# A lambda-shaped attention followed by a SoLU mixture layer: the last unit's feed-forward input side whole, its output side in halves with tiles of their own, and a new order of all steps

## The chip, the cores and the metric

The kernel runs on one core of one Trainium2 chip. Its time is the device time of one execution in microseconds (us); lower is better. The core has five engines that work side by side, each taking its own instructions in order: PE (matrix products and transposes), DVE (elementwise work on vectors), ACT (activation functions, with a scale and a bias), POOL (elementwise work, slower for most of it) and SP (it only issues transfers). ACT and POOL can issue transfers too. SBUF is the memory of 128 partitions that all engines read and write; PSUM is the small one that PE writes its results to.

## What is computed

Attention over 4 sequences of 768 positions with 8 heads of width 64, then a feed-forward layer of 1024 inner columns on the 3072 rows of 512 columns that come out. Of each row of scores only 8 global columns and the last 96 positions are kept, and each head has a bias that falls off with distance:

```python
scores = scale * np.matmul(q, k.transpose(0, 1, 3, 2))
is_global = pos[None, :] < int(n_global)              # n_global = 8
is_local = (rel >= 0) & (rel < int(n_local))          # n_local = 96
scores = scores + bias[None, :, :, :]                 # -slope of the head * distance
scores = np.where(is_global | is_local, scores, -1000000000.0)
a = np.exp(scores - max); a = a / (sum + 1e-09); x = a @ v
h = x @ w_in
solu = h * softmax(h)
ln = (solu - mean) / sqrt(var + 1e-06) * g_ln
out = ln @ w_out
```

## The kernel before

**Units and rows.** The 3072 rows are cut into 12 units of 256: unit u is sequence u // 3 and stretch u % 3 of it. A unit has two halves r of 128 rows in the feed-forward part.

**The order is written out.** The string ORDER lists 670 steps, one word each, and the kernel issues them in that order; nothing is rescheduled. Each engine gets its own instructions in the order of the words, and an engine that waits holds everything of its own that stands behind. A word is a name and its arguments; the letter after the name is the engine or the issuing queue (S is SP, A ACT, P POOL, D DVE). The pools of tiles give out slots when a step asks for a tile, and that step waits until the slot's last reader is done. What holds work up most is in PSUM: three slots called big, for scores (sc), sums (lb), values (pa) and the inner columns (ph), and two called small, for transposes (qturned, kturned, lT), global scores (gs), outputs (po), pv and the warm-up products.

**The attention steps of a unit.** `q`, `k`, `v` load 256 KB halves into 13 staging slots; `cq`, `ck`, `cv` cast them to 16 bits (cast, lines 138, 140 and 142 for ACT, DVE, POOL); `tq`, `tk` transpose on PE (L301) and `eq`, `ek` copy the result out of PSUM; `gk` picks the global keys (POOL, L315). `S:u:g` are the scores of a pair of heads (L324), `X` their exponentials on ACT (L333), `M` the product with the mask on DVE (L340), `gS` and `gX` the same for the global columns (L353, L361), `gv0` and `gv` the global values (POOL L366; PE L370 and DVE L373). `L` sums on PE (L384, L393), `I` inverts the sums on ACT in two instructions (L401, L402), `V` multiplies by the values (L412, L422) and `N` normalises into xT on DVE (L430).

**The feed-forward steps of half r of unit u.** `A:u:r` is the product with w_in into ph (L446, 8 products of 512 columns), `E` its exponential on ACT with the sum s0 (L460), `U` e times ph on DVE with the sum s1 (L468), `Q` the sum of squares s2 on ACT (L477), `Z` the scale rs from s0, s1 and s2 in five small POOL instructions (L492 to L499), `d` the transpose of un by a transfer on SP's queue into uT (L516; three slots), `O` the product with the scaled w_out into po (L522), `o` the scaling of po by rs into osb on DVE (L534) or ACT (L536), `st` the store (L543), whole units of 512 KB but for unit 11. w_out is loaded with `wo`, scaled with `sc`, its mean is taken (`mean`, `cm`) and removed (`ce` on DVE, L578; `pr` and `sm` on POOL, L590 and L594). `warm:n` are n products of zeros on PE (L230) that nothing reads.

**The last unit.** Unit 11 is worked in halves throughout: A, E, U and Q have a third argument, the half of the 1024 inner columns; its transposes go over PE (`t`, L505) and a copy (`e`) instead of a transfer; its outputs are stored in quarter units. The halves of one step write two halves of the same tile (one ph, one e, one un, one lT, one uT, one osb). Z then first adds the two partial sums of each kind (L488).

The units end in the order 8, 7, 11, 10, 9: the last words are those of unit 9's outputs and stores, with 18 warm-up products after the last output.

Of the kernel before, what the change touches and what calls it, by code (L numbers as in the profile page):

```python
# [26 lines left out]
q:S:0:0 k:S:1:0 k:S:0:0 off:1 off:0 zero dist:1 mask:1:0 mask:1:4 id cap dist:0 mask:0:2 mask:0:1  # L27
mask:0:5 mask:0:4 k:S:0:1 ck:P:0 tk:0 ek:D:0 q:S:0:1 cq:P:0 tq:0 k:S:1:1 ck:P:1 q:S:1:0 gb tk:1
ek:D:1 q:S:1:1 q:S:2:0 q:S:2:1 cq:D:2 mask:1:5 mask:0:0 mask:1:1 mask:0:6 mask:1:6 mask:1:3 eq:A:0
mask:0:3 S:0:0 gk:0 S:0:2 gS:0 X:0:0 X:0:2 S:0:3 k:S:3:0 S:0:1 X:0:1 cq:P:1 gX:0 fill hm X:0:3  # L30
k:S:2:0 k:S:2:1 ck:P:2 mask:1:7 mask:1:2 mask:0:7 tq:1 eq:D:1 tq:2 S:1:2 X:1:2 S:1:0 X:1:0 eq:D:2
M:0:3 gS:1 M:0:0 gX:1 S:1:1 X:1:1 v:S:0:0 S:1:3 tk:2 ek:A:2 q:S:4:0 q:S:4:1 cq:D:4 v:S:0:1 M:1:0
selV X:1:3 k:S:3:1 ck:D:3 wi:0 M:0:1 S:2:1 X:2:1 S:2:3 X:2:3 cv:P:0 S:2:0 gS:2 gX:2 gv0:0 X:2:0
M:0:2 M:1:2 S:2:2 k:S:4:0 k:S:4:1 tq:4 eq:A:4 M:1:3 tk:3 ek:D:3 gk:1 ck:A:4 X:2:2 L:0 I:0 M:1:1
# [629 lines left out]
```

The softmax here doesn't subtract the row's maximum and nothing guards it: scores larger than these inputs give would overflow.

## Time and profile before

| | |
|---|---|
| time, median of 3 runs | 174.66 us (174.57 to 175.02) |
| the profiled execution: its own time | 174.96 us |
| its span, first to last instruction | 173.2 us |
| busy: PE, ACT, DVE, POOL | 154.9, 144.5, 127.3, 91.4 us |
| granted PE clock over the span | 0.98 |
| moved by transfers | 34.35 MB, mean 198 GB/s |
| first transpose on PE; first product of the feed-forward part (A:0:0) | 8.00 us; 36.2 us |
| end of the last output (O:9:1); last store landed; last warm-up product ended | 168.4; 171.85; 172.3 us |

The busy shares are over the whole span. PE is busy almost without a break between 36 and 168 us, so what counts there is PE's idle time and what PE is given to do that nothing reads. A step's place in the trace is found by counting its instructions on its engine.

### The profile page before, as it was taken

How to read it: one execution, taken by the hardware profiler on the slowest of the kernel's cores; microseconds unless marked ns; L12 is line 12 of the kernel's file. 1: busy time of each engine (PE TensorE's matmuls, PEld its weight loads, DVE VectorE, ACT ScalarE, POOL GpSimd, SP SyncE). 2: the span in 40 equal slices, each digit the busy share in tenths (PEclk: the TensorE clock that was granted, in tenths of full speed). 3: DMA queues.
4: the chain of work that ended last, by engine and by line, in shares of the span. 5: the costliest groups of instructions: out<-in, count | busy, mean ns of one | idle time of the engine just before them, and what ended most of it. 6: DMA issues, size and time to landing. Idle time of an engine off the chain costs nothing.

```text
span 173.2 us, 4093 instructions
## 1 busy us (share of the span) xinstructions
PE 154.9 (89%) x1551; PEld 86.1 (50%) x1551; DVE 127.3 (73%) x200; ACT 144.5 (83%) x232; POOL 91.4 (53%) x195
## 2 busy tenths in 40 slices
PE   0179599899999989997999999999999958998997
PEld 0156375655654545436455655555545634454443
DVE  5079978999899989929989899869837672475310
ACT  5959999899999997769999899999895566796540
POOL 5276809300814998987288987882210001464760
PEclk9999759999999999999999999999999999999999
DMA  4999999999999998689999692398753530055354
GB/s 138 309 346 310 328 255 244 256 354 287 312 341 162 221 109 166 111 249 234 360 206 155 147 217 98 121 264 224 167 140 74 169 125 0 0 164 139 68 162 198
DMA packets 52532, 34.35 MB, mean 198 GB/s; under 512 B 43169, under 2 KB 43681, under 8 KB 52513
## 3 DMA queue, kind: packets, MB, share of 16 engines
q1 hardware_dynamic: 48784, 27.14, 63.9%
q0 software_dynamic: 1984, 5.77, 13.9%
q10 hardware_dynamic: 1744, 1.18, 2.5%
q8 instruction: 12, 0.20, 0.5%
q14 instruction: 8, 0.06, 0.1%
HBM read 23.07 MB, written 6.29 MB: 169 GB/s over the span
## 4 chain that ended last, share of the span: by engine, by line
PE 66%; POOL 10%; DVE 5%; DMA 5%; ACT 5%; issue 5%; SPq 4%; POOLq 0%; DVEq 0%; ACTq 0%
PE ph L446 21%; PE po L522 20%; PE lb L393 5%; PE pa L412 4%; PE warm L230 4%; SPq L157 4%; PE sc L324 3%; DMA q<-in_q_dram 3%; PE qturned L301 3%; POOL gw L594 2%; DMA v<-in_v_dram 2%; PE kturned L301 2%; DVE q L140 2%; ACT pt L333 2%; PE pa L422 1%
## 5 line engine op out<-in xcount | busy, mean ns | idle before, releaser
L446 PE MATMUL ph<-w_in,xT 128*128 128x512 f16 x192 | 44.9, 379 | 3.1 <-DVE un L468 2.3
L522 PE MATMUL po<-gw,uT 128*128 128x512 f16 x192 | 44.5, 379 | 0.0
L333 ACT ACTIVATE pt<-sc 128x896 f16<-128x896 f32 (+1 forms) x48 | 40.0, 871 | 2.2 <-PE sc L324 2.0
L468 DVE SCALAR_TENSOR_TENSOR un<-e,ph 128x1024 f16<-128x1024 f16 (+1 forms) x26 | 29.1, 1135 | 8.5 <-ACT e L460 7.6
L340 DVE TENSOR_TENSOR pt<-pt,mask 128x896 f16<-128x896 f16 (+1 forms) x48 | 28.3, 614 | 5.5 <-ACT pt L333 5.5
L446 PEld LDWEIGHTS <-xT 128*128 128x128 f16 x192 | 17.8, 98 | 24.0 <-issue 2.6
L460 ACT ACTIVATE e<-ph 128x1024 f16<-128x1024 f32 (+1 forms) x26 | 24.8, 955 | 4.5 <-PE ph L446 2.8
L522 PEld LDWEIGHTS <-uT 128*128 128x128 f16 x192 | 17.9, 98 | 20.9 <-issue 0.5
L477 ACT ACTIVATE sq<-un 128x1024 f16<-128x1024 f16 (+1 forms) x26 | 25.7, 990 | 2.0 <-DVE un L468 1.8
L497 POOL TENSOR_SCALAR w<-s,w 128x1 f32<-128x1 f32 x22 | 6.8, 311 | 32.3 <-ACT sq L477 30.6
L324 PE MATMUL sc<-qT,kT 64*128 64x128 f16 (+2 forms) x256 | 15.9, 246 | 3.0 <-ACT kT L138 1.8
L430 DVE TENSOR_TENSOR xT<-pa,rlb 128x1024 f16<-128x1024 f32 x12 | 14.6, 1221 | 2.9 <-ACT rlb L402 1.6
L301 PE MATMUL kturned<-ident,k 128*128 128x128 f16 x96 | 8.8, 246 | 8.0 <-POOL k L142 8.0
L495 POOL TENSOR_SCALAR w<-mean,w 128x1 f32<-128x1 f32 x24 | 14.5, 605 | 2.4
L499 POOL TENSOR_TENSOR rs<-w,neghalf 128x1 f32<-128x1 f32 x24 | 14.6, 610 | 2.0
L140 DVE COPY kT<-kturned 128x1024 f16<-128x1024 f16 x9 | 11.0, 1222 | 6.0 <-PE kturned L301 6.0
L534 DVE TENSOR_SCALAR osb<-po,rs 128x512 f32<-128x512 f32 (+1 forms) x15 | 10.7, 711 | 5.8 <-DMA out_dram<-osb 3.0
L401 ACT ACTIVATE rlb<-lb 128x1024 f32<-128x1024 f32 x12 | 12.4, 1032 | 3.0 <-PE lb L393 2.8
L536 ACT ACTIVATE osb<-po,rs 128x512 f32<-128x512 f32 (+1 forms) x11 | 7.1, 650 | 8.5 <-PE po L522 4.5
L324 PEld LDWEIGHTS <-kT 64*128 64x128 f16 x256 | 9.3, 100 | 8.3 <-issue 4.6
L402 ACT ACTIVATE rlb<-rlb 128x1024 f32<-128x1024 f32 x12 | 12.7, 1057 | 0.4
L301 PEld LDWEIGHTS <-k 128*128 128x128 f16 x96 | 7.1, 111 | 10.1 <-POOL k L142 8.2
(88 smaller groups left out, 230.2 us busy)
## 6 DMA issues: line engine op xcount, KB each, us to landing
out_dram<-osb SPq DMA_DIRECT2D x11, 512.0 KB, 2.9
q<-in_q_dram SPq DMA_DIRECT2D x19, 256.0 KB, 5.2
k<-in_k_dram SPq DMA_DIRECT2D x18, 256.0 KB, 5.3
v<-in_v_dram SPq DMA_DIRECT2D x16, 256.0 KB, 6.3
v<-in_v_dram POOLq DMA_DIRECT2D x7, 256.0 KB, 5.0
k<-in_k_dram POOLq DMA_DIRECT2D x6, 256.0 KB, 8.2
w_out<-in_moe_w_out_dram SPq DMA_DIRECT2D x3, 512.0 KB, 6.1
q<-in_q_dram POOLq DMA_DIRECT2D x5, 256.0 KB, 8.6
```

Source lines behind the costliest of these rows:

```text
L301: nc.tensor.transpose(out=t[:, r], in_=src[:, r].rearrange("p m d -> p (m d)"), identity=held["ident"])
L324: nc.tensor.matmul(out=sc[:, m, o : o + e - a], lhsT=held["kT", u - s + j // 2][r, g, ts(j % 2, P)], rhs=qT[r, g, a:e], start=True, stop=True,
L333: nc.scalar.activation(out=pt[:, :, 0:w], in_=held.pop(("sc", u, g))[:, :, 0:w], func=AF.Exp, scale=inv_sqrt_d)
L340: nc.vector.tensor_tensor(out=pt[:, :, 0:w], in0=pt[:, :, 0:w], in1=held["mask"][:, g, :, o : o + w], op=ALU.mult)
L430: nc.vector.tensor_tensor(out=xT.rearrange("p g (r i) -> p g r i", r=2), in0=held.pop(("pa", u)).rearrange("p g (i r) -> p g r i", r=2), i ...
L446: nc.tensor.matmul(out=held["ph", t][:, ts(fh, 512)], lhsT=held["xT", t[0]][:, j, ts(t[1], P)], rhs=held["w_in"][:, j, ts(fh, 512)], start ...
L460: nc.scalar.activation(out=held["e", t][:, f], in_=held["ph", t][:, f], func=AF.Exp, accum_out=s0)
L468: nc.vector.scalar_tensor_tensor(out=held["un", t][:, f], in0=held["e", t][:, f], scalar=1.0, in1=held["ph", t][:, f], op0=ALU.mult, op1=A ...
L477: nc.scalar.activation(out=sq[:, f], in_=held["un", t][:, f], func=AF.Square, accum_out=s2)
L495: eng.tensor_scalar(out=w2, in0=mean, scalar1=mean, scalar2=w1, op0=ALU.mult, op1=ALU.subtract)
L499: eng.tensor_tensor(out=rs, in0=w3, in1=held["neghalf"], op=ALU.pow)
L522: nc.tensor.matmul(out=held["po", t], lhsT=held["uT", t][:, c, :], rhs=held["gw"][:, c, :], start=(c == 0), stop=(c == NFC - 1),)
```

## The change

Four things are edited.

First, A, E, U, Q and Z of unit 11 are no longer cut: `A:11:0`, `A:11:1` and so on do the same as those of any other unit, and the additions of partial sums go. Second, the halves that remain of unit 11 are cut as before (`t`, `e` and `O` by inner columns, `o` and `st` by output columns), but each half of lT and of uT is a tile of its own, and each half of the scaled outputs is a tile osbh of its own in the three slots of osb. Third, some steps change engine or queue: the scalings `o` of 2:1, 3:1, 4:1, 5:1, 7:1, 8:1, 10:1 and 11:0:0 go from DVE to ACT, those of 1:0, 5:0 and 9:1 from ACT to DVE; k of unit 10 and v of units 8 and 11 are cast by ACT instead of DVE, and q of unit 11, v of unit 10 and the copy of q of unit 7 go the other way; k of unit 0 is cast by DVE instead of POOL, q of unit 2 by POOL instead of DVE, v of unit 2 by DVE instead of POOL; of the loads, k:0:0 and v:0:0 go to ACT's queue, q:10:0, q:10:1, k:10:0, k:11:1 and v:7:1 to POOL's, and k:7:1, k:8:0, q:7:0, q:9:0, v:10:0 and v:8:1 from POOL's to SP's. Fourth, all words stand in a new order. PE's order differs from the old by swaps among neighbours but for the start and the last 40 us.

The edited functions:

```diff
-    def ff_in(t, h=None):
-        if ("ph", t) not in held:
-            held["ph", t] = big("ph").rearrange("p a f -> p (a f)")
+    def ff_in(t):
+        held["ph", t] = big("ph").rearrange("p a f -> p (a f)")
         for j in range(NCC):
-            for fh in (0, 1) if h is None else (h,):
+            for fh in (0, 1):
...
-        if halves:
-            for x in (s0, s1, s2):
-                both = col("both")
-                eng.tensor_tensor(out=both, in0=x[0], in1=x[1], op=ALU.add)
-                x[0] = both
...
     def ff_turn(t, h=None):
-        if ("lT", t) not in held:
-            held["lT", t] = small([P, NFC, P], FP16, "lT")
-        for c in range(NFC)[part(h, NFC)]:
+        cs = range(NFC)[part(h, NFC)]
+        lT = held["lT", t, h] = small([P, len(cs), P], FP16, "lT")
+        for i, c in enumerate(cs):
...
     def ff_evac(engine, t, h=None):
-        c = part(h, NFC)
-        if ("uT", t) not in held:
-            held["uT", t] = msb.tile([P, NFC, P], FP16, name="uT", bufs=3)
-        cast(engine, held["uT", t][:, c], held["lT", t][:, c])
+        lT = held.pop(("lT", t, h))
+        uT = held["uT", t, h] = msb.tile([P, lT.shape[1], P], FP16, name="uT", tag="uT", bufs=3)
+        cast(engine, uT, lT)
...
     def ff_scale(engine, t, h=None):
         u, r = t
-        c = part(h, D_MODEL)
-        if ("osb", u) not in held:
-            held["osb", u] = msb.tile([P, 2, D_MODEL], FP32, name="osb", tag="osb", bufs=3)
+        if h is not None:
+            to = held["osb", t, h] = msb.tile([P, D_MODEL // 2], FP32, name="osbh", tag="osb", bufs=3)
+        else:
+            if ("osb", u) not in held:
+                held["osb", u] = msb.tile([P, 2, D_MODEL], FP32, name="osb", tag="osb", bufs=3)
```

The order, in the four stretches that matter below (lines of ORDER before and after):

```diff
-q:S:0:0 k:S:1:0 k:S:0:0 off:1 off:0 zero dist:1 mask:1:0 mask:1:4 id cap dist:0 mask:0:2 mask:0:1
-mask:0:5 mask:0:4 k:S:0:1 ck:P:0 tk:0 ek:D:0 q:S:0:1 cq:P:0 tq:0 k:S:1:1 ck:P:1 q:S:1:0 gb tk:1
+gb k:A:0:0 off:1 dist:1 mask:1:5 mask:1:6 mask:1:3 mask:1:7 mask:1:1 cap off:0 id dist:0 mask:0:3
+mask:1:0 mask:0:0 mask:0:1 mask:1:4 v:A:0:0 mask:1:2 mask:0:7 mask:0:5 fill k:S:0:1 ck:D:0 tk:0
+k:S:1:0 q:S:0:0 q:S:0:1 cq:P:0 tq:0 k:S:1:1 ck:P:1 ek:D:0 zero gk:0 eq:A:0 mask:0:2 q:S:2:0 tk:1
...
-M:0:2 M:1:2 S:2:2 k:S:4:0 k:S:4:1 tq:4 eq:A:4 M:1:3 tk:3 ek:D:3 gk:1 ck:A:4 X:2:2 L:0 I:0 M:1:1
-gv:0 k:P:6:0 tk:4 q:S:3:0 q:S:3:1 ek:D:4 cq:D:3 L:1 I:1 warm:5:3 M:2:3 tq:3 eq:D:3 v:S:1:0 v:S:1:1
+M:1:3 M:1:0 ck:A:4 v:S:0:1 cv:P:0 gv0:0 tk:3 k:P:6:0 S:2:2 X:2:2 cq:D:4 tq:4 eq:A:4 M:2:1 M:1:1
...
-N:3 cv:D:4 S:5:3 X:5:3 S:5:1 X:5:1 gS:5 gX:5 sc:P:3 mean cm cq:D:7 S:6:3 X:6:3 ce:0 ce:1 ce:2
-d:S:0:0 V:4 N:4 ce:3 ce:4 pr:7 k:P:7:1 S:5:2 Q:0:1 ck:D:7 v:P:7:0 tq:7 eq:A:7 X:5:2 pr:5 sm:5 sm:6
-sm:7 d:S:1:0 v:S:5:0 v:S:6:0 v:S:6:1 A:3:0 E:3:0 Z:P:1:1 U:3:0 A:4:0 E:4:0 U:4:0 Q:2:1 O:0:0
-o:A:0:0 tk:7 ek:D:7 S:6:2 X:6:2 S:6:1 X:6:1 M:5:3 cq:D:8 M:5:0 gk:2 Z:P:0:1 S:6:0 Z:P:1:0 X:6:0
-O:1:0 M:5:2 cv:D:6 M:5:1 Q:3:0 M:6:2 S:7:2 S:7:0 gS:7 gX:7 o:A:1:0 A:3:1 d:S:1:1 X:7:0 X:7:2 M:7:2
-v:S:5:1 k:S:9:1 Q:4:0 ck:D:9 d:S:0:1 M:6:0 cv:D:5 O:1:1 o:A:1:1 E:3:1 d:S:2:0 k:S:10:0 U:3:1 M:6:3
-q:S:10:0 q:S:11:0 O:0:1 o:A:0:1 gS:6 gX:6 S:7:1 X:7:1 L:5 I:5 q:P:9:0 gv0:2 gv:2 tq:8 M:6:1 eq:D:8
-q:P:9:1 d:S:3:0 V:5 N:5 S:7:3 M:7:1 tk:9 ek:D:9 X:7:3 Q:2:0 Q:3:1 Z:P:2:1 Z:P:2:0 q:S:10:1 v:P:9:0
-k:S:10:1 v:S:9:1 st:S:0 A:4:1 E:4:1 M:7:0 U:4:1 M:7:3 A:5:1 E:5:1 U:5:1 L:6 I:6 gS:8 Z:P:3:1 O:2:0
+gX:5 Q:1:0 sc:P:3 mean cm S:6:3 X:6:3 N:3 pr:7 cv:D:4 k:P:7:0 v:P:7:0 cq:D:7 ce:0 ce:1 V:4 N:4
+ce:2 ce:3 ce:4 d:S:0:0 S:5:3 X:5:3 Q:0:1 Q:2:1 tq:7 eq:D:7 gk:2 A:3:0 S:5:2 X:5:2 q:S:8:0 k:S:7:1
+ck:D:7 E:3:0 U:3:0 A:4:0 E:4:0 d:S:1:0 d:S:1:1 pr:5 sm:5 sm:6 sm:7 O:0:0 o:A:0:0 U:4:0 tk:7 ek:D:7
+v:S:6:0 Q:3:0 v:S:5:0 S:6:0 S:6:2 X:6:0 X:6:2 O:1:0 gS:7 gX:7 S:6:1 X:6:1 S:7:0 S:7:1 Z:P:1:1
+Z:P:1:0 Z:P:0:1 o:D:1:0 M:5:0 M:5:1 v:S:6:1 M:6:1 cv:D:6 M:5:3 M:6:0 M:5:2 d:S:0:1 X:7:0 X:7:1
...
+Z:P:3:0 v:P:9:0 M:7:3 A:5:1 E:5:1 U:5:1 d:S:2:0 q:S:11:0 q:S:11:1 O:2:0 tk:9 k:S:11:0 V:6 Q:3:1
+Z:P:3:1 Q:4:1 d:S:3:1 st:S:0 d:S:3:0 d:S:2:1 v:S:10:0 k:S:10:1 d:S:4:0 v:S:9:1 v:S:11:0 N:6 S:8:0
+X:8:0 Z:P:4:1 o:D:2:0 L:7 I:7 q:P:10:0 q:P:10:1 cv:D:7 A:6:0 ek:D:9 gS:8 gX:8 E:6:0 v:P:11:1 V:7
+S:8:3 X:8:3 ck:A:10 v:P:8:0 v:S:8:1 k:P:11:1 gk:3 U:6:0 N:7 O:3:0 o:D:3:0 M:8:0 Q:6:0 v:P:10:1
+Z:P:4:0 Z:P:2:1 O:3:1 o:A:3:1 cq:D:10 S:8:2 X:8:2 M:8:2 S:8:1 Q:5:1 X:8:1 d:S:4:1 st:S:1 d:S:6:0
+M:8:3 A:7:0 tq:9 E:7:0 tq:10 eq:A:10 cq:D:11 eq:D:9 ck:D:11 U:7:0 A:5:0 E:5:0 U:5:0 tk:10 ek:A:10
...
-V:11 N:11 O:7:1 V:10 N:10 gX:9 L:9 I:9 Z:P:7:1 o:D:7:1 V:9 N:9 d:S:8:0 d:S:8:1 A:11:0:0 E:11:0:0
-U:11:0:0 A:11:0:1 E:11:0:1 Q:8:0 Z:P:8:0 A:11:1:0 A:11:1:1 A:10:0 Q:11:0:0 E:11:1:0 E:10:0
-E:11:1:1 U:11:0:1 U:11:1:0 st:S:5 U:10:0 A:9:0 E:9:0 U:9:0 U:11:1:1 O:8:0 o:A:8:0 Q:10:0 O:8:1
-Z:P:8:1 o:D:8:1 t:11:0:0 e:D:11:0:0 A:10:1 t:11:0:1 e:D:11:0:1 st:S:7 d:S:10:0 Z:P:10:0 O:11:0:0
-Q:11:0:1 Q:9:0 E:10:1 U:10:1 Q:11:1:0 Z:P:11:0:1 O:11:0:1 o:D:11:0:0 o:A:11:0:1 Q:11:1:1
-Z:P:11:1:1 A:9:1 t:11:1:0 e:D:11:1:0 t:11:1:1 e:D:11:1:1 st:A:11:0:1 E:9:1 O:10:0 o:A:10:0
-O:11:1:0 U:9:1 O:11:1:1 o:D:11:1:0 st:S:8 Q:10:1 o:A:11:1:1 d:S:9:0 O:9:0 Q:9:1 st:A:11:1:1
-Z:P:9:0 st:S:11:0:0 st:A:11:1:0 Z:P:10:1 d:S:10:1 o:A:9:0 O:10:1 o:D:10:1 d:S:9:1 O:9:1 Z:P:9:1
-o:A:9:1 st:S:10 warm:5:2 warm:4:4 st:S:9 warm:4:5 warm:5:1
+cv:D:10 L:11 I:11 Z:P:7:0 M:9:3 o:D:7:0 d:S:8:0 M:9:1 V:10 N:10 V:11 N:11 L:9 I:9 V:9 N:9 A:11:0
+E:11:0 U:11:0 Q:8:0 Q:8:1 A:10:1 E:10:1 U:10:1 A:11:1 A:10:0 E:11:1 E:10:0 U:10:0 d:S:10:0 Z:P:8:0
+Z:P:8:1 O:8:0 o:A:8:0 O:7:1 o:A:7:1 Q:10:0 Z:P:10:0 O:8:1 o:A:8:1 Q:11:0 Z:P:11:0 U:11:1 t:11:0:0
+st:S:7 A:9:0 t:11:0:1 e:D:11:0:0 O:11:0:0 e:A:11:0:1 O:11:0:1 O:10:0 E:9:0 o:A:11:0:0 t:11:1:0
+e:D:11:1:0 U:9:0 o:A:11:0:1 Q:11:1 Z:P:11:1 o:A:10:0 Q:10:1 A:9:1 E:9:1 Z:P:10:1 t:11:1:1 st:S:8
+Q:9:0 e:D:11:1:1 O:11:1:0 O:11:1:1 o:A:11:1:1 d:S:10:1 O:10:1 o:A:10:1 st:S:11:0:1 st:S:11:0:0
+warm:4:4 d:S:9:0 U:9:1 Q:9:1 d:S:9:1 Z:P:9:0 st:S:11:1:1 o:D:11:1:0 st:A:11:1:0 Z:P:9:1 O:9:0
+o:A:9:0 O:9:1 o:D:9:1 warm:5:2 warm:4:5 st:S:10 warm:5:1 st:S:9
```

## The prediction, made before the changed kernel ran

> **What bounds the kernel now.** I read the page's slices first (who is full, and when), then the busy times by stage, then PE's idle time with what ended it, then the chain, and last the order of the tail. The slices, and the busy times by stage (columns: the stage, its length, busy us of PE, of its weight loads, of DVE, ACT and POOL, granted clock, share of the transfer engines, GB/s):
>
> ```profile
> PE   0179599899999989997999999999999958998997
> ACT  5959999899999997769999899999895566796540
> DMA  4999999999999998689999692398753530055354
> ```
>
> ```profile
> 0.00:36.20 36.20, 23.89 (x314) 16.95 (x314) 27.17 (x45) 31.01 (x48) 18.97 (x41) 0.91 0.99 278
> 62.00:80.00 18.00, 15.83 (x124) 7.58 (x123) 14.13 (x24) 14.85 (x26) 16.16 (x27) 1.00 0.87 169
> 80.00:107.00 27.00, 27.00 (x299) 15.27 (x296) 25.01 (x36) 26.35 (x41) 19.69 (x41) 1.00 0.99 210
> 107.00:134.40 27.40, 27.40 (x289) 14.40 (x288) 20.29 (x32) 24.03 (x36) 11.48 (x27) 1.00 0.64 158
> 134.40:168.40 34.00, 31.14 (x235) 15.77 (x228) 16.88 (x31) 22.16 (x45) 13.53 (x43) 1.00 0.36 99
> ```
>
> From 36.2 us on PE is the bound: 27.00 of 27.00, 27.40 of 27.40. It idles in two stages alone, 62 to 80 (2.2 us) and the tail (2.9 us). Before 36.2 the loads (share 0.99) and ACT (31 of 36) decide. So the question is what the new order does to the start of PE's packed stretch, to those idle times, and whether it makes new ones. The waits behind the idle times (engine, tile and line, what it waited for: total us, times, longest):
>
> ```profile
> PE ph L446 <- DVE un L468: 2.3, 1, 2.3
> PE gs L353 <- ACT osb L536: 1.3, 1, 1.3
> PE ph L446 <- DVE xT L430: 0.7, 1, 0.7
> PE lT L505 <- DVE uT L140: 0.5, 1, 0.5
> ```
>
> The first is A:11:0:1. It waits for U:11:0:0, though it reads nothing of it: both halves write one ph.
>
> ```profile
> 142.66 0.68 DVE L468 SCALAR_TENSOR_TENSOR un<-e,ph 128x512 f16<-128x512 f16 x1
> ...
> 143.40 6.20 PE L446 MATMUL ph<-w_in,xT 128*128 128x512 f16 x28 [2.34 <-DVE un L468]
> ```
>
> The second comes from POOL. In the chain, the scale of O:1:0 ends at 74.93, ACT's scaling stands waiting for it with everything of ACT behind:
>
> ```profile
> 72.16 1.62 POOL w L495
> ...
> 74.36 0.57 POOL rs L499
> 74.93 0.02 issue
> 74.95 0.03 ACT osb L536
> 74.98 0.56 issue
> 75.54 1.72 ACT pt L333 x2
> ```
>
> The third is A:4:0, behind N:4 on DVE, which stands behind three `ce`. The fourth is t:11:1:1, which shares lT and uT with the other half.
>
> **The change part by part.** PE's products are the same in number and size, so PE gives nothing but its waits. The sum is made against the profiled execution, 174.96 us (span 173.2 and 1.76 around it), which is 0.30 above the median of 174.66.
>
> *The start, -1.0 (-1.8 to +0.6).* k:0:0 goes out on ACT's queue beside SP's first, so q:0:1 is the fourth issue on SP, not the fifth; an issue there takes 0.60 with 0.04 between, and cq:P:0 followed that load at once (landed 8.30, cast 8.43). That is 0.64 for q, S:0 and ACT's first exponential. k:0 is cast on DVE (0.69 such casts) instead of POOL (1.04). Against it: ACT has one mask more ahead of eq:A:0 (0.47, in ACT's idle 1.72 there), DVE has gb's five small instructions (0.8) ahead of dist, and POOL gets cq:P:2 (1.04) but loses ck:P:0 (1.04). Later, ck:A:6 began at 37.40 when its load landed at 37.34 (ACT idle 1.01 after it); the new order issues k:6 ahead of gk:1 and its 4.8 us wait, so that wait goes. Best: 0.64 + 1.01 and the cast's 0.35, some -1.8; worst, the loads are full anyway and the mask and gb are paid, 0.47 + 0.15: +0.6. I take -1.0, the middle, since the stage is bound by loads and ACT in turn.
>
> *A:4:0, -0.8 (-0.9 to 0).* N:4 stands behind two `ce` instead of three (0.74), and V:4 ends in time for it. PE lost 0.90 there by the spacing of its products. DVE pays `ce` and eq:D:7 (1.23) after it: see gS:7.
>
> *O:0:1 to gS:6, -1.4 (-1.5 to +0.3).* PE lost 1.50. Z:1:0 is now second of the three scales, not third (the one it passes took 2.03 from 68.27 to 70.30), gk:2 (0.47) is ahead of `sm`, and o:1:0 is on DVE, so ACT does not stand idle (2.21) on it. Next late is DVE, which holds M:5 behind o:D:1:0; L:5 needs M:5:2 only after O:1:1, A:3:1 and O:0:1 (5.2 us of PE) against 4.4 us of DVE.
>
> *gS:7, +0.5 (0 to +1.4), new.* It takes the small slot of tk:7, free when ek:D:7 is done, and DVE has ahead of that ce:2 to ce:4 (2.2), eq:D:7 (1.23), ck:D:7 (0.69), U:3:0 and U:4:0 (1.22 each). Laid end to end from N:4's end, that is some 1.4 later than now against PE's place; the 0.9 of A:4:0 and the head's lead are inside it.
>
> *Unit 10's loads, +1.0 (0 to +5.6), new.* k:S:10:1 now stands on SP behind d:S:2:1, which waits until O:2:0 gives its uT slot back (about 86); it was issued at 78.0. q:10 is issued by POOL behind Z:4:1, so after Q:4:1 (91.9 now, some 3 earlier then), at about 91. Loads of this stretch land 5.0 (v on POOL, median) to 8.6 (q on POOL) after issue: 96 to 99.7. DVE reaches cq:D:10 at about 95.5 and holds behind it M:8:2, M:8:3, cq:D:11, eq:D:9, ck:D:11, U:7:0, U:5:0 (6.2 us); S:10:0 needs U:5:0's slot at 103.9. The last DVE end is 102.6 to 106.6, so PE waits 0 to 2.7; 1.0 is nearer the POOL median of this stretch. With the longest landing of any transfer (10.1) and 1.5 more on POOL it is 5.6.
>
> *ACT, +0.3 (0 to +1.2).* Seven full scalings come (0.60 apart), three go, two half copies and scalings come, and unit 11 whole saves 0.8: +2.7 on 144.5. In 107 to 134 ACT has 3.4 to spare; in 80 to 107 only 0.65, and there come two (1.2), less what ACT no longer stands idle before (2.2).
>
> *The tail, -2.0 (-2.4 to +1.0).* From the end of L:11 (134.4) to the end of O:9:1 (168.4) is 34.0 now, of it 2.5 lost before A:11:0:1 and 0.7 before t:11:1:1. In the new order warm:4:4 stands before O:9:0, 0.86 more on PE. I laid it end to end from L:11's end with the rows (A and O 1.73, V 1.13, N 1.23, the two of I 2.1, E and Q 1.1, U 1.22, a scaling 0.69, a transpose by transfer 3.1 from issue to use): A:11:0 starts at 4.0 with N:11 done at 3.6; A:11:1 at 7.5 (N:9 6.7); O:8:0 at 10.95; A:9:0 at 16.4; O:10:0 at 20.1; A:9:1 at 22.05; t:11:1:1 at 23.8 (o:A:10:0, which also waits for the landing of st:S:8, 22.75); O:10:1 at 25.75 (d:10:1 issued at 21.9, landed 25.0); O:9:0 at 28.35 (d:9:0 28.05); O:9:1 at 30.1 (d:9:1 29.5), end 31.8. No wait on PE, but the last two have 0.3 and 0.6 to spare, so I give 0.2 back: 32.0. Worst, E:9:1 and both transposes come 3 us late behind o:A:10:0: +1.0.
>
> *The end, -0.35 (-0.5 to +0.2).* Eighteen warm-up products run for 3.9 after O:9:1 and the last store landed 3.4 after it. With fourteen (3.0) the store is last; o:9:1 on DVE takes 0.06 longer than on ACT.
>
> What hides the rest: the removed Z additions lie on POOL, whose chain is off the end; osbh tiles take slots freed by stores that landed long before, but for o:A:9:0, which waits for st:11:1:1 (31.0, while O:9:1 still runs).
>
> Sum: -1.0 - 0.8 - 1.4 + 0.5 + 1.0 + 0.3 - 2.0 - 0.35 = -3.75; 174.96 becomes 171.2, and beside the median 170.9.
>
> A page speaks against the move of loads to POOL. Row: loads of q issued on POOL took 8.6 us to land, on SP 5.2. The Trainium skill, "SBUF — State Buffer", section "SBUF: two separate sides", says that POOL writes the descriptors of its own transfers and cannot while a DVE copy in a fast mode holds the port pair that they share. Its example is 620 ns becoming 3100. By that, 2.5 more on q:10, the sum would be -1.3 and the time 173.4; by the rows, which hold such waits already, it stays.
>
> **The rivals.**
>
> *ACT takes the lead back.* ACT is 26.35 of 27.00 busy in 80 to 107, so a PE that comes early only waits for exponentials. For: the row. Against: ACT stood idle for 4.2 just before, and the new order ends that. Then only tail and end remain, -2.35: 172.3, up to 174.1 with the 0.3 and 0.5 and the 1.0 on top.
>
> *The tail does not gain.* d:9:0 and d:9:1 wait for slots of uT that the halves of unit 11 hold, and land late; 0.3 of slack is little beside 3.0 to 10.1 of landing. The transfer engines are at 0.36 there, where transposes landed in 3.1. If each comes 1 later: -1.7 to -2.0 in all, 172.9.
>
> *Slower: unit 10's loads.* One mechanism: PE and DVE stand at q:10 and k:10 around 97 because their loads were queued behind POOL's scales and SP's d:2:1. My sum holds 1.0 of it; from 4.75 on (loads landing after about 101) it eats all gains. At its bound of 5.6, with the head's gain lost as well, -3.75 + 4.6 + 1.0: 176.5. For: the transfer engines are 0.99 busy there. Against: of the loads then in flight most landed within 7.
>
> **How the numbers follow.** No change and a measurable one part at about 0.3% (174.1 to 175.2). The forecast has 0.55; ACT as the limit 0.17 (0.13 faster, 0.04 the same); the tail without gain 0.08 (0.06 and 0.02); unit 10's loads 0.20, slower. Faster 0.74, the same 0.06, slower 0.20. The forecast's own range is 168.4 (head, both idle times and tail near their best ends) to 172.9; the range of all reaches to 175.4.
>
> **What would show it.** Right: PE's first ff product near 35; no idle before the whole A:11 products; gS:6 and A:4:0 without waits; L:11's end to O:9:1's near 32; the last store after the last warm-up product. Wrong: idle of PE before tq:10 or S:10 with a load as the cause; POOL's scales stretched (2.24 was the longest) with DVE behind o:D:1:0; idle before O:9:0.

## The result, and the profile after

The changed kernel took 175.08 us (median; 174.94 to 175.34) beside 174.62 us (174.57 to 175.02) of the kernel before on the same chip: ratio 1.0023, 95% interval 1.0004 to 1.0043. The forecast was 170.9. The time lies above the forecast's own range (168.4 to 172.9) and near the upper end of the range of all outcomes (175.4), on the other side of the kernel before.

The table goes by marks before which PE has done the same steps in both orders: the start of L:3, the start of A:4:0, the end of L:11, the end of O:9:1, and the end of the span. Each cell after the first is the change of that stage's length against the profile of before, in us. The last column belongs to an experiment below, in which only words of the order were moved; its profile is of the fastest of six runs (169.95 us), and its median of 171.2 is some 4.5 us under the kernel before by the ratio.

| stage (length before) | predicted | changed kernel | eleven words moved |
|---|---|---|---|
| start to L:3 (45.09) | -1.0 | +4.03 | -1.69 |
| L:3 to A:4:0 (19.60) | -0.8 | -0.79 | -0.70 |
| A:4:0 to L:11's end (69.72) | -1.4 +0.5 +1.0 +0.3 = +0.4 | -0.96 | -0.65 |
| L:11's end to O:9:1's end (34.03) | -2.0 | -2.29 | -2.02 |
| O:9:1's end to the span's end (4.81) | -0.35 | +0.07 | +0.06 |
| sum | -3.75 | +0.06 | -5.00 |

The stage up to A:4:0 and the tail came within 0.3 us of the forecast, the one between them better, the end gave nothing, and the start ate all of it. The slices of the changed kernel's page (40 of 4.33 us, busy tenths):

```profile
PE   0294598896899999999999998999999999999995
...
ACT  5984899784999999998999898999789969689740
...
DMA  4947999999999781299969999927873930081763
```

Before, the transfers were full from the second slice to the fifteenth; now there is a hole in the third and fourth, and ACT has one in the fourth and one in the tenth. From the twelfth slice to the last but one PE shows a 9 in every slice but one. The busy times by stage (same columns as in the prediction, and the stage 36.2 to 62, in which PE was busy for 25.75 before) say the same: the idle time of 62 to 80 and of the tail is gone, and what is new lies before 62, but for 0.55 us in 80 to 107.

```profile
0.00:36.20 36.20, 23.24 (x290) 15.64 (x290) 26.66 (x44) 29.60 (x45) 18.29 (x39) 1.00 0.91 263
36.20:62.00 25.80, 23.49 (x265) 13.57 (x264) 22.25 (x34) 22.70 (x36) 6.62 (x13) 1.00 1.12 269
62.00:80.00 18.00, 17.89 (x151) 8.99 (x150) 17.83 (x26) 17.40 (x30) 16.25 (x28) 1.00 0.58 131
80.00:107.00 27.00, 26.45 (x308) 15.15 (x307) 23.64 (x36) 25.49 (x40) 19.85 (x39) 1.00 1.07 219
107.00:134.40 27.40, 27.40 (x261) 14.25 (x260) 19.86 (x31) 24.99 (x38) 10.92 (x30) 1.00 0.72 162
134.40:168.40 34.00, 34.00 (x277) 17.62 (x276) 14.59 (x23) 26.71 (x46) 14.90 (x42) 1.00 0.51 137
```

PE's waits on others (total us, times, longest), the ones that are new:

```profile
PE qturned L300 <- POOL q L141: 3.8, 2, 2.2
...
PE ph L444 <- ACT pt L332: 1.8, 1, 1.8
...
PE lb L383 <- DVE un L461: 0.4, 1, 0.4
```

The 2.2 is the transpose tq:2, the 1.8 is A:1:1, the 0.4 is L:2. Both longer ones lead back to transfers. First tq:2, in the timeline of the first 18 us (start, length, engine, line, operation; xN joins N of one kind, with the time between them):

```profile
4.06 7.90 SPq L156 DMA_DIRECT2D q<-in_q_dram  x4
4.73 0.43 ACTq L162 DMA_DIRECT2D v<-in_v_dram  x1
...
12.01 1.25 SPq L156 DMA_DIRECT2D k<-in_k_dram  x2
...
15.58 1.03 PE L300 MATMUL qturned<-ident,q 128*128 128x128 f16 x8 [2.25 <-POOL q L141]
```

Four loads of q take SP 7.90 us, though an issue takes 0.60. The same row in the kernel before, then the two loads on each side of the hole in the changed kernel:

```profile
4.71 2.54 SPq L157 DMA_DIRECT2D q<-in_q_dram  x4
```

```profile
4.71 1.25 SPq L156 DMA_DIRECT2D q<-in_q_dram  x2
11.43 0.54 SPq L156 DMA_DIRECT2D q<-in_q_dram  x1
```

The fourth, q:2:1, is issued at 11.43, after 5.47 us in which SP issues nothing. That is 0.02 after v:0:0 landed (11.41), the load that ACT had issued at 4.73 while the other queues' loads were moving. q:2:1 landed at 14.37, in the kernel before at 11.80.

Then A:1:1, in the chain that ended last (start, length, what):

```profile
30.76 9.85 DMA q<-in_q_dram
40.61 0.02 issue
40.63 0.02 ACTq L549
40.65 0.04 issue
40.69 0.37 ACTq L549
...
41.14 0.37 issue
41.51 1.06 ACT k L137
...
42.74 0.81 ACT pt L332
43.55 1.01 ACT e L456 x2
```

q:5:0 lands at 40.61; only then ACT issues wo:0 (L549), behind which stand the cast of k:6 (L137) and X:4:3, the exponential (L332) whose end at 43.55 frees the slot for A:1:1. ACT stood idle for 3.01 us there. The table of waits puts that idle time down to DVE's cast of k:8, which ended about then (41.03); the chain names the transfer. The two readings needed an experiment.

The theory: each transfer signals its landing on one of eight semaphores (counters that an engine can wait for), which are given out in turn, nearly in the order of the words, over SP's and ACT's queues together. The next transfer on the same semaphore, eight or nine such transfers later in the words, waits for that landing, also if it stands on another queue; and it holds its own queue meanwhile. The traces name the semaphore of each transfer, and the pairs: q:2:1 with v:0:0 (nine transfers on), wo:0 with q:5:0 (eight). In each of the fourteen traces of this case SP and ACT use eight semaphores and POOL eight others. Of the 1243 times that SP or ACT used one again, the issue came after the landing before it every time. So a load that starts late on a busy queue and lands late stops another queue. The rivals: the new order of loads and casts is worse in itself; 256 KB more among the first loads are the cost, whatever queue carries them; ACT waited for DVE.

The Trainium skill, "Perfetto Trace Analysis", section "DMA Instruction — HWDGE (DVE, Sync)", bears on another reading of SP's hole, that SP and ACT hold each other up while their descriptors are made. It says that the time shown for an issue starts once its semaphores are satisfied, and includes the wait for the unit that makes descriptors. The trace agrees: the hole has no instruction in it, and q:2:1's issue behind it, 0.02 after the landing on its semaphore, took 0.54. By that page the hole is a wait for a semaphore.

### The profile page after: what moved, and what is told of

Read it like the earlier page. It is cut to its first block, busy times and chain, and to the rows that moved or that the text cites. A ratio compares the mean times of both kernels' runs of the same rounds, so it can differ in the third digit from the quotient of the medians.

```text
span 173.3 us, 4070 instructions
## 1 busy us (share of the span) xinstructions
PE 155.5 (90%) x1551; PEld 86.4 (50%) x1551; DVE 125.6 (72%) x190; ACT 146.9 (85%) x230; POOL 86.8 (50%) x188
## 4 chain that ended last, share of the span: by engine, by line
PE 60%; DMA 14%; DVE 10%; ACT 8%; issue 3%; POOL 1%; SPq 1%; ACTq 0%; DVEq 0%; POOLq 0%
PE po L506 20%; PE ph L444 15%; DMA q<-in_q_dram 8%; DMA v<-in_v_dram 6%; PE pa L411 5%; DVE pt L339 4%; PE lb L392 4%; PE warm L229 4%; DVE un L461 4%; PE sc L323 3%; PE qturned L300 3%; ACT e L456 2%; ACT sq L469 2%; ACT pt L332 2%; PE pa L421 2%
## 5 line engine op out<-in xcount | busy, mean ns | idle before, releaser
L506 PE MATMUL po<-gw,uT 128*128 128x512 f16 x192 | 43.9, 379 | 0.0
L332 ACT ACTIVATE pt<-sc 128x896 f16<-128x896 f32 (+1 forms) x48 | 39.6, 865 | 3.3 <-PE sc L323 3.3
L461 DVE SCALAR_TENSOR_TENSOR un<-e,ph 128x1024 f16<-128x1024 f16 x24 | 29.0, 1218 | 10.9 <-ACT e L456 9.1
L339 DVE TENSOR_TENSOR pt<-pt,mask 128x896 f16<-128x896 f16 (+1 forms) x48 | 30.2, 660 | 4.8 <-ACT pt L332 4.8
L456 ACT ACTIVATE e<-ph 128x1024 f16<-128x1024 f32 x24 | 24.4, 1020 | 1.9 <-PE ph L444 1.2
L469 ACT ACTIVATE sq<-un 128x1024 f16<-128x1024 f16 x24 | 25.2, 1051 | 0.1
L482 POOL TENSOR_SCALAR w<-s,w 128x1 f32<-128x1 f32 x24 | 9.3, 389 | 26.5 <-ACT sq L469 24.8
L139 DVE COPY qT<-qturned 128x1024 f16<-128x1024 f16 x9 | 11.0, 1218 | 5.4 <-PE qturned L300 5.4
L523 ACT ACTIVATE osb<-po,rs 128x512 f32<-128x512 f32 x13 | 8.9, 688 | 5.3 <-PE po L506 3.3
L300 PE MATMUL qturned<-ident,q 128*128 128x128 f16 x96 | 8.9, 250 | 3.9 <-POOL q L141 3.8
```

Source lines behind the costliest of these rows:

```text
L139: nc.vector.tensor_copy(out=out, in_=in_)
L300: nc.tensor.transpose(out=t[:, r], in_=src[:, r].rearrange("p m d -> p (m d)"), identity=held["ident"])
L332: nc.scalar.activation(out=pt[:, :, 0:w], in_=held.pop(("sc", u, g))[:, :, 0:w], func=AF.Exp, scale=inv_sqrt_d)
L339: nc.vector.tensor_tensor(out=pt[:, :, 0:w], in0=pt[:, :, 0:w], in1=held["mask"][:, g, :, o : o + w], op=ALU.mult)
L456: nc.scalar.activation(out=held["e", t], in_=held["ph", t], func=AF.Exp, accum_out=s0)
L461: nc.vector.scalar_tensor_tensor(out=held["un", t], in0=held["e", t], scalar=1.0, in1=held["ph", t], op0=ALU.mult, op1=ALU.mult, accum_out=s1,
```

## The experiments

All ratios are to the kernel before, run beside each kernel on the same chip. Three chips took turns, the first four kernels on one, the next four on another, the last four on a third. The kernel before scatters more on them than beside the result (174.5 to 176.9, and one run of 179.2), so times a few tenths of a per cent apart can't be told from each other there; profiles can. The order below is not that of the runs.

**v of unit 0 loaded late.** The word v:A:0:0 goes, and v:S:0:0 stands ahead of v:S:0:1.

```diff
-mask:1:0 mask:0:0 mask:0:1 mask:1:4 v:A:0:0 mask:1:2 mask:0:7 mask:0:5 fill k:S:0:1 ck:D:0 tk:0
+mask:1:0 mask:0:0 mask:0:1 mask:1:4 mask:1:2 mask:0:7 mask:0:5 fill k:S:0:1 ck:D:0 tk:0
...
-ck:A:4 v:S:0:1
+ck:A:4 v:S:0:0 v:S:0:1
```

> The changed kernel, but the first half of v of unit 0 is issued by SP just ahead of its second half, not by ACT at the start. Theory: SP stood idle for 5.47 us (5.96 to 11.43) because the load q:2:1 may only be issued when v:0:0, two words from the start and eight transfers ahead of it, has landed (11.41). With v:0:0 gone from there, SP has no idle above 0.5 in the first 12 us, q:2:1 lands near 11.5 instead of 14.37, PE's wait of 2.25 before tq:2 goes, A:1:0 starts near 35.5 instead of 37.7, and of these 2.3 about 2 are left at the end: 173.0 us (172.0 to 174.0). Rival: the head is late because the new order of loads and casts is worse in itself (k:0 cast on DVE, q:2 on POOL, five instructions of gb first): A:1:0 stays near 37.5 and the time within 0.5 of 175.1.

Measured: 170.82 us, ratio 0.973 (0.968 to 0.978). SP issues without a hole in the first 13 us, q:2:1 lands at 10.79, PE's wait before tq:2 is gone, A:1:0 starts at 35.36. The gain is larger than the theory's 2: also A:1:1 and L:2 wait no more, because q:5:0, with all loads earlier, landed at 35.65 instead of 40.61 (in the changed kernel its own issue took 4.41 us on SP; why is not shown).

**The same load at the same place, by SP.** One letter is changed.

```diff
-mask:1:0 mask:0:0 mask:0:1 mask:1:4 v:A:0:0 mask:1:2
+mask:1:0 mask:0:0 mask:0:1 mask:1:4 v:S:0:0 mask:1:2
```

> The changed kernel with the same load of v:0:0 at the same place in the order, issued by SP instead of ACT. It is then SP's first load (the other seven of the head are 0.64 later each) and lands near 5, long before the transfer eight places behind it is issued. Theory (SP waits for a landing that comes late): no idle of SP above 1 us, q:2:1 lands near 12.5, time 173.4 us (172.4 to 174.4), a little above the kernel that issues v:0:0 late. Rival (256 KB more among the first loads, on whatever queue, is what delays the head): q:2:1 lands near 14 and the time is 175.1 or above (174.7 to 176).

Measured: 170.77 us, ratio 0.972 (0.967 to 0.977). v:0:0 is first on SP and lands at 4.08. The four loads of q in SP's timeline:

```profile
4.56 2.55 SPq L155 DMA_DIRECT2D q<-in_q_dram  x4
```

The same bytes, as early as before, cost nothing. The rival of the bytes is out; so is that of the casts, since ck:D:0, cq:P:2 and gb stand unchanged.

**The kernel before with only that load moved to ACT.** Its word goes behind the masks, and these words ahead of SP's first load, which changes no queue's order but for v:0:0.

```diff
-q:S:0:0 k:S:1:0 k:S:0:0 off:1 off:0 zero dist:1 mask:1:0 mask:1:4 id cap dist:0 mask:0:2 mask:0:1
-mask:0:5 mask:0:4 k:S:0:1
+off:1 off:0 zero dist:1 mask:1:0 mask:1:4 id cap dist:0 mask:0:2 mask:0:1 mask:0:5 mask:0:4 v:A:0:0
+q:S:0:0 k:S:1:0 k:S:0:0 k:S:0:1
...
-X:1:1 v:S:0:0 S:1:3
+X:1:1 S:1:3
```

> The kernel before, with only v:0:0 moved to ACT's queue, behind the masks, and in the order ahead of SP's first load, so that SP's eighth load (q:1:1) is the one that comes eight transfers after it. Theory: SP stands idle from about 5.3 until v:0:0 has landed (about 10 to 11.5), all loads behind are 2 to 5 us later, PE's first product of the feed-forward part at about 38 instead of 36.2, time 176.5 us (175.5 to 178). Rival (the queue of v:0:0 has no part in the head's delay): 174.6 (174.2 to 175.1).

Measured: 178.9 us, ratio 1.019 (1.014 to 1.025). Again four loads of q take SP so long; v:0:0 landed at 11.34 and q:1:1 was issued at 11.35:

```profile
4.71 8.47 SPq L156 DMA_DIRECT2D q<-in_q_dram  x4
```

One moved load alone makes the old kernel 1.9% slower (1.4 to 2.5), where about 1.1% was expected.

**Only the places of words.** SP's first eleven loads are written ahead of v:A:0:0. SP's and ACT's own orders are as in the changed kernel.

```diff
-mask:1:0 mask:0:0 mask:0:1 mask:1:4 v:A:0:0 mask:1:2 mask:0:7 mask:0:5 fill k:S:0:1 ck:D:0 tk:0
-k:S:1:0 q:S:0:0 q:S:0:1 cq:P:0 tq:0 k:S:1:1 ck:P:1 ek:D:0 zero gk:0 eq:A:0 mask:0:2 q:S:2:0 tk:1
+mask:1:0 mask:0:0 mask:0:1 mask:1:4 k:S:0:1 k:S:1:0 q:S:0:0 q:S:0:1 k:S:1:1 q:S:2:0 q:S:1:0 q:S:1:1
+q:S:2:1 k:S:2:0 k:S:2:1 v:A:0:0 mask:1:2 mask:0:7 mask:0:5 fill ck:D:0 tk:0 cq:P:0 tq:0 ck:P:1
...
```

> The changed kernel with its eleven first SP loads (k:0:1 to k:2:1) written ahead of the word v:A:0:0 instead of behind it. No engine's and no queue's own order changes by that: SP issues the same loads in the same order, ACT issues v:0:0 behind the same masks. Only the place of v:0:0 among the words moves, by eleven transfers, so that the load that may go only when v:0:0 has landed is no longer q:2:1 but q:3:0, ten loads later on SP. Theory (the eight marks of transfers are given out by the order of the words, over all queues): SP's idle of 5.5 us before q:2:1 goes, v:0:0 has landed (about 11.5) before q:3:0 is due (about 13), and the time is that of the kernels that load v:0:0 by SP: 2.9% under the changed kernel (2.0 to 3.5). Rival (ACT's queue itself is what holds SP's loads, or v:0:0 landing late holds other work): the same as the changed kernel, within 0.5%.

Measured: 171.2 us, ratio 0.974 (0.969 to 0.979); the profiled execution took 169.95 (span 168.2). The slices and the timeline of the head:

```profile
PE   0388599999999999999999989999999999999995
...
DMA  4999999999999930999859999848936900364863
```

```profile
4.06 2.54 SPq L155 DMA_DIRECT2D q<-in_q_dram  x4
6.65 1.25 SPq L155 DMA_DIRECT2D k<-in_k_dram  x2
6.88 0.41 ACTq L161 DMA_DIRECT2D v<-in_v_dram  x1
```

The hole of the transfers in slices 3 and 4 is gone, with the same instructions in the same order on every queue. Beside the changed kernel on the same chip (0.9955, below) that is 2.2% less, within the expected 2.0 to 3.5. This settles the theory's main point. It also shows the rule from the other side: v:0:0 now goes at 6.88, 0.02 after q:0:1 landed (6.86), the transfer it now has to wait for; it landed at 13.42, later than expected, and q:3:0, which shares its semaphore, was issued at 13.78. The one hole of SP above 0.4 near there, 0.92 before v:0:1, is a wait for a load of SP's own (k:2:1, landed 13.29).

**Four words only.** SP's first four loads ahead of v:A:0:0, so that q:4:1 is the one that waits.

```diff
-mask:1:4 v:A:0:0 mask:1:2 mask:0:7 mask:0:5 fill k:S:0:1 ck:D:0 tk:0
-k:S:1:0 q:S:0:0 q:S:0:1 cq:P:0
+mask:1:4 k:S:0:1 k:S:1:0 q:S:0:0 q:S:0:1 v:A:0:0 mask:1:2 mask:0:7 mask:0:5 fill ck:D:0 tk:0 cq:P:0
```

> The changed kernel with only SP's first four loads written ahead of the word v:A:0:0, so that the load which may go only when v:0:0 has landed (about 11.4) is q:4:1, the third load behind q:2:1 on SP. No queue's own order changes. Theory: SP reaches q:4:1 at about 8.6 and stands idle for 2.8 us there, half of the 5.5 of the changed kernel; q:2:1 lands near 11 and PE's wait before tq:2 goes, but all loads from q:4:1 on are some 2.2 later than where eleven words were moved, of which part reaches PE: ratio to the kernel before 0.980 (0.974 to 0.988). Rival (only q:2:1 was on the path, the later loads have slack): the same as with eleven words moved, 0.974 (0.969 to 0.979).

Measured: 173.38 us, ratio 0.986 (0.980 to 0.992), as the theory had it and above the rival's bounds. The two loads of q:4 in SP's timeline have the hole between them; v:0:0 landed at 11.89, q:4:1 went at 11.91:

```profile
8.09 4.36 SPq L155 DMA_DIRECT2D q<-in_q_dram  x2
```

The hole is 3.1 us (8.82 to 11.91) instead of 5.5, and A:1:0 starts at 36.84, between 34.61 and 37.74. q:2:1 landed at 12.56, not near 11, and PE still waited 0.51 before tq:2 where it had waited 2.25. So the whole stream of loads counts, not q:2:1 alone.

**The changed kernel again,** on the chip of the kernel with eleven words moved, of the second run below and of the tail alone.

> The changed kernel itself, so that the others of this call can be set against it on one chip. Its ratio to the kernel before should again lie near 1.002 (0.998 to 1.007).

Measured: 175.5 us (173.71 to 176.79), ratio 0.9955 (0.9912 to 0.9997). That misses the expected bounds by a little, on the other side of 1 than the first comparison. By their intervals the two together allow anything from 0.9% less to 0.4% more; by their middles it is under half a per cent either way.

**wo:0 issued by SP.** This asks what ACT's 3.01 us were.

```diff
-wo:A:0 v:S:4:0 v:S:4:1 ck:D:8 q:P:6:0 q:P:6:1 ck:A:6
+wo:S:0 v:S:4:0 v:S:4:1 ck:D:8 q:P:6:0 q:P:6:1 ck:A:6
```

The first time:

> The changed kernel with one eighth-share load of w_out, wo:0, issued by SP at its place instead of by ACT. Theory: ACT's idle of 3.01 us before ck:A:6 (38.5 to 41.5) is the wait of that load in ACT's own queue for q:5:0, eight transfers before it (landed 40.61); with it on SP ACT goes on, X:4:3 starts near 40 instead of 42.6, PE's waits of 1.80 before A:1:1 and 0.38 before L:2 go, and 0.5 to 2 of it is left at the end: 174.0 us (173.0 to 174.7). Rival (the profile's own reading: ACT waits for the cast of k of unit 8 on DVE, that ended at 41.03): the idle stays at 3 and the time within 0.4 of 175.1.

Measured: 172.77 us, ratio 0.985 (0.980 to 0.991), a little below the expected bounds. The second time:

> The changed kernel with wo:0 issued by SP, a second time, for a clean profile beside the changed kernel itself. Theory: the first wait stays (2.2 us before tq:2), the second goes (no idle of PE before A:1:1 and L:2), so the time is 1.0 to 2.0% under the changed kernel of this call, by more than the 2.2 us of the second wait at most if ACT, then ahead, saves something later. Rival: it is the same as the changed kernel within 0.4%, and the first measurement was one of another chip.

Measured: 172.98 us, ratio 0.983 (0.978 to 0.988), beside 0.9955 of the changed kernel: 1.3% less, 2.2 us. ACT's timeline (35 to 41 us) of the second:

```profile
35.82 3.12 ACT L331 ACTIVATE pt<-sc 128x896 f16<-128x896 f32 x4
38.83 1.05 ACT L136 ACTIVATE k<-k 128x1024 f16<-128x1024 f32 x1
...
39.95 0.92 ACT L331 ACTIVATE pt<-sc 128x896 f16<-128x896 f32 x1
```

The cast of k:6 follows the exponentials at once, although DVE's cast of k:8 ended at 41.21, no earlier than in the changed kernel. So ACT had not waited for DVE; it had stood at its own transfer. PE has no wait before A:1:1 and L:2, and the wait before tq:2 stays (1.76). O:9:1 ends at 166.36 instead of 168.43: nearly all of the 1.80 and 0.38 of the second wait is left at the end.

**The tail alone, in the old order.** Unit 11's input side whole, the halves of its output side in own tiles, all words as before.

```diff
-V:9 N:9 d:S:8:0 d:S:8:1 A:11:0:0 E:11:0:0 U:11:0:0 A:11:0:1 E:11:0:1 Q:8:0 Z:P:8:0 A:11:1:0 A:11:1:1
+V:9 N:9 d:S:8:0 d:S:8:1 A:11:0 E:11:0 U:11:0 Q:8:0 Z:P:8:0 A:11:1
...
```

> The kernel before in its own order, with only the last unit's input side whole (A, E, U, Q and Z of unit 11) and the halves of its output side in tiles of their own; nothing else is moved. Theory: of PE's waits the 2.3 before A:11:0:1 goes (the whole A:11:0 needs no U first) and the 0.5 to 0.7 before t:11:1:1 too, less up to 0.5 because E:11:0 starts 0.86 later: the tail from the end of L:11 to the end of O:9:1 is 31.5 to 32.3 instead of 34.0, the time 1.2% under the kernel before (0.8 to 1.6). Rival (the tail is as long because d:9:0 and d:9:1, not A:11, decide when O:9 can run, and only the new order moved them): 34.0 stays, within 0.4%.

Measured: 174.98 us, ratio 0.9965 (0.9934 to 0.9996); L:11's end to O:9:1's end is 34.31. The rival's numbers came, but not as it was put: the waits before A:11 and t:11:1:1 went, as the theory had it, and others took their place. PE's timeline near the end:

```profile
156.96 3.61 PE L505 MATMUL po<-gw,uT 128*128 128x512 f16 x16 [0.29 <-DVE uT L138]
161.98 1.90 PE L505 MATMUL po<-gw,uT 128*128 128x512 f16 x8 [1.40 <-DMA uT<-un]
164.07 1.90 PE L505 MATMUL po<-gw,uT 128*128 128x512 f16 x8 [0.19 <-DMA uT<-un]
166.87 1.89 PE L505 MATMUL po<-gw,uT 128*128 128x512 f16 x8 [0.90 <-DVE osb L520]
```

O:9:0 waits 1.40 for d:9:0, whose slot of uT comes free only with O:10:0 (ended 158.85; d:9:0 issued 158.88), now that each half of unit 11 takes a slot of its own. O:9:1 waits 0.90 for a slot of po. The profile names o:10:1 on DVE (ended 166.81), and the trace's semaphores agree: the first product of O:9:1 waits for the one that DVE signals with o:10:1 (166.83), not for ACT's, on which o:9:0 (ended 166.60, after 1.81 us of waiting for a quarter store) is signalled.

**The old head with the new tail.** The old order up to L:11 (and four steps that the new order had done by then), the new one behind it.

```diff
-L:11 I:11 V:11 N:11 O:7:1 V:10 N:10 gX:9 L:9 I:9 Z:P:7:1 o:D:7:1 V:9 N:9 d:S:8:0 d:S:8:1 A:11:0:0
+gX:9 Z:P:7:1 d:S:8:1 st:S:5 L:11 I:11 d:S:8:0 V:10 N:10 V:11 N:11 L:9 I:9 V:9 N:9 A:11:0
...
```

> The kernel before in its own order up to L:11, and from there the changed kernel's order (with unit 11's input side whole and its halves in tiles of their own); four steps that the changed order had done earlier stand just ahead of L:11. Theory: the tail's gain needs the new order beside the new tiles, since in the old order O:9:0 waited 1.41 us for d:9:0 and O:9:1 0.90 for po's slot (o:A:9:0 behind the landing of a quarter store). With both, L:11's end to O:9:1's end is 31.6 to 32.3 instead of 34.0, time 1.2% under the kernel before (0.9 to 1.6). Rival (the tail of the changed kernel is short only because its head leaves less work on ACT and DVE at L:11): above 33.3, at most 0.5% under.

Measured: 172.27 us, ratio 0.983 (0.979 to 0.988), a little more than the expected 0.9 to 1.6%; L:11's end to O:9:1's end is 31.89, within its bounds. PE's timeline:

```profile
157.83 3.62 PE L505 MATMUL po<-gw,uT 128*128 128x512 f16 x16
161.28 1.03 PE L228 MATMUL warm<-zeros 128*128 128x512 f16 x4
162.28 3.61 PE L505 MATMUL po<-gw,uT 128*128 128x512 f16 x16
165.73 3.18 PE L228 MATMUL warm<-zeros 128*128 128x512 f16 x14
```

No wait is left. The tail's gain is real and does not need the new head. The new tiles alone do not give it, as the run before shows; the new order with the old tiles was not run.

**Without the warm-up products of the end,** in the kernel with eleven words moved.

```diff
-warm:4:4 d:S:9:0 U:9:1 Q:9:1 d:S:9:1 Z:P:9:0
+d:S:9:0 U:9:1 Q:9:1 d:S:9:1 Z:P:9:0
...
-o:A:9:0 O:9:1 o:D:9:1 warm:5:2 warm:4:5 st:S:10 warm:5:1 st:S:9
+o:A:9:0 O:9:1 o:D:9:1 st:S:10 st:S:9
```

> The kernel with eleven words moved, without the four warm-up products ahead of O:9:0 and without the fourteen after O:9:1 (products of zeros that nothing reads). Theory: O:9:0 starts when d:9:0 has landed (159.70 where warm:4:4 ended at 159.76), so the four were free to within 0.1, and the end is set by the last store's landing and about 1.3 us behind it, so the fourteen were free too: same time within 0.2%, span's end 1.2 to 1.4 after the last landing as before. Rival (by the working of the prediction, where warm:4:4 stood on PE's path with 0.86 and the trailing products set the end when the store lands before them): 0.86 to 1.2 us less, a ratio 0.5 to 0.7% lower.

Measured: 171.75 us (169.71 to 173.56), ratio 0.977 (0.971 to 0.983), not to be told from 0.974. PE then waits where it had multiplied zeros:

```profile
160.86 3.63 PE L505 MATMUL po<-gw,uT 128*128 128x512 f16 x16 [0.73 <-DMA uT<-un]
```

The tail is 31.65, against 32.01 with them: the four had cost at most 0.36, not 0.86. The last store landed at 168.01 and the span ended 1.35 later, as it does with the fourteen in the kernel with eleven words moved (1.35): there they set nothing. In this profile wo:0 went at 36.81, 0.07 after q:5:0's landing (36.74), and A:1:1 waited 0.85 and L:2 0.38; so in the kernel with eleven words moved the second wait is short, but can come back.

**The last store in two,** in the kernel with eleven words moved: `held["osb", u][:, r]` of 256 KB for each half.

```diff
+        elif h is None:
+            queues[queue].dma_start(out=rows[:, r], in_=held["osb", u][:, r])
...
-o:A:9:0 O:9:1 o:D:9:1 warm:5:2 warm:4:5 st:S:10 warm:5:1 st:S:9
+o:A:9:0 O:9:1 o:D:9:1 warm:5:2 warm:4:5 st:S:10 st:S:9:0 warm:5:1 st:S:9:1
```

> The kernel with eleven words moved, and the last store (unit 9, 512 KB) as two of 256 KB, one for each half, so that the last one carries half the bytes. Theory: the end is the last landing and about 1.3 us, and a quarter store of 128 KB landed 1.8 to 2.0 after its issue where 512 KB took 2.6, so 256 KB lands 0.3 earlier: ratio to the kernel before 0.972 (0.967 to 0.977). Rival: a landing has a fixed time, nothing is gained or 0.1 is lost by the other issue on SP.

Measured: 170.34 us (169.62 to 171.97), ratio 0.973 (0.968 to 0.979). Its stores, by size (KB each, median us from issue to landing):

```profile
out_dram<-osb SPq DMA_DIRECT2D x2, 256.0 KB, 2.0
out_dram<-osbh SPq DMA_DIRECT2D x3, 128.0 KB, 2.2
```

The last 256 KB landed 2.00 after its issue, the 512 KB of the kernel with eleven words moved 2.61; from O:9:1's end to the last landing it is 2.87 against 3.52. That is more than the expected 0.3, which had taken 1.8 to 2.0 us for 128 KB; in the kernel with eleven words moved those stores took 2.05 to 2.66. The runs are too scattered to show these 0.65 us in the time. This kernel and those with v:0:0 moved (or the words around it) are some 2.7% faster than the kernel before, and faster than the changed one.

## Why the prediction was wrong, and where it was right

*The start failed.* The step: "k:0:0 goes out on ACT's queue beside SP's first, so q:0:1 is the fourth issue on SP, not the fifth", and the bounds -1.8 to +0.6 made of it. What it says came: tq:0 started at 8.41 instead of 9.52. But v:0:0, the other load that goes to ACT's queue, was listed among the changes and given no price. It cost 5.5 us of SP's issues and, through the later loads, 5.7 us at L:3 (+4.03 against -1.69 with eleven words moved, where only its place among the words differs; the medians of the two kernels on one chip are 4.3 us apart). With its place mended the term came out at -1.69, inside the bounds of the prediction. "The loads are full anyway" was taken as the worst case; worse was that they stand still.

*ck:A:6 failed, as a part of the same term.* "So that wait goes" was right of the load (k:6 landed at 36.07), but ahead of ck:A:6 stood wo:0, whose wait had moved with the words from a load that had landed in time (30.21, with wo:0 issued at 35.71) to q:5:0. The "1.01" of idle time on ACT stands in no row of the profile before: ACT was idle for 0.12 ahead of that cast and not at all behind it. 0.12 became 3.01. The term's own sums slip too: 0.64, 1.01 and 0.35 make 2.0, not 1.8, and the middle of -1.8 and +0.6 is -0.6, not -1.0.

*A:4:0 and gS:6 were right.* Both wait no more, as the profile's lists of waits show; the stage up to A:4:0 gave 0.79 for 0.8. *gS:7* cost 0.1 and not 0.5. *Unit 10's loads* were given 1.0; no wait of PE leads back to them. q:10:0 and q:10:1, which POOL issued, landed 3.6 us after their issues (95.35 to 98.91, 95.99 to 99.65), before their cast began (100.61). PE's one wait there is for ACT's copy eq:A:10:

```profile
105.88 0.61 PE L300 MATMUL kturned<-ident,k 128*128 128x128 f16 x8 [0.44 <-ACT qT L137]
```

The Trainium skill, "SBUF — State Buffer", section "SBUF: two separate sides", had been weighed against the rows on the loads of q (8.6 us on POOL, 5.2 on SP): by that page POOL cannot write descriptors while DVE holds the port pair that they share. No run here shows it; in the changed kernel loads of q on POOL landed after 4.6 us (median), on SP after 4.8.

*ACT* cost those 0.44 where 0.3 was forecast: the chain runs over ACT alone from 100.3 to 105.8, with o:3:1 (0.69), which the change moved there, in it. As a rival it did not take the lead back: in 80 to 107 it is busy for 25.49 instead of 26.35, and PE is at 26.45 of 27.00. *The tail* was right: 31.74 where 32.0 was forecast, with O:9:0 starting at 164.81 as warm:4:4 ended (164.84) and d:9:0 had landed (164.71). The slack of 0.3 that the prediction had worked out there came as 0.1; the experiment with the old order shows what happens without it.

*The end failed.* "With fourteen (3.0) the store is last" came: the last store landed at 171.95, the last product of zeros ended at 171.45. What the term left out is what SP does behind it. At its end SP waits for one semaphore after the other. Its instructions of that kind, before and after (count, ns of the shortest, median and longest, first and last start):

```profile
L659 SPq EVENT_SEMAPHORE  x3: 17/17/487, 171.9 to 173.2; - x3
```

```profile
L647 SPq EVENT_SEMAPHORE  x10: 17/28/28, 172.0 to 173.2; - x10
```

Before, the last store's semaphore stood last, and beside it the wait for the last product: the 487 ns end at 172.36, the product ended at 172.32, and the span ends 0.92 after it. So there the trailing products did set the end. In the changed kernel the last store's semaphore stands first, and seven more waits, some 0.06 apart, follow its landing: the span ends 1.36 after it, against 0.91 in the old head with the new tail, where it stands last again. What the fewer products gave, the longer list took: the term came out at +0.07.

Of the rivals none happened as it was told. Slower by one mechanism was foreseen, at another place.

## What to carry to other kernels

Where one program's words are dealt out to several queues, count the transfers of SP and ACT together in the order of the words (POOL's had semaphores of their own here): a transfer that lands late holds up another eight or nine transfers on, whichever of the two queues that one stands on. So put the word of a load where its landing fits its neighbours', above all one issued by a busy compute engine, and price an "extra early load" by the queue that it may stop, not only by its bytes. In the trace the sign is a hole in a queue that ends up to 0.1 us after another queue's landing.

## What was not expected of the hardware

A queue's stop at another queue's landing is exact. SP went on 0.01 to 0.02 after v:0:0 had landed in six kernels (11.43 after 11.41, 11.91 after 11.89, 11.30 after 11.28, 11.35 after 11.34, 14.63 after 14.61, 14.11 after 14.10), and ACT issued wo:0 0.07 to 0.10 after q:5:0's landing in seven (40.69 after 40.61, 34.84 after 34.77, 35.75 after 35.65, 36.08 after 36.00, 36.81 after 36.74, 37.20 after 37.12, 36.48 after 36.41). The kernel before has such a stop too: SP issued nothing from 40.87 to 43.11, until v:2:1, which ACT had issued at 33.07, had landed (43.04); what it costs was not measured. The idle time of the compute engine behind such an issue can be put down to an unrelated engine: 3.01 us stood as a wait for DVE, and the chain of waits had it right.
